# Batch 1's Fourier folds shared by two engines, with its last output a step sooner, and batch 0's q and k transposed in the banks of P

## The chip, the cores and the metric

The kernel runs on one core of a Trainium2 chip. The metric is the device time of one execution in microseconds (us). A core has five engines that run beside each other, each with its own queue of instructions in program order: PE (TensorE, matrix products), ACT (ScalarE), DVE (VectorE), POOL (GpSimd) and SP (SyncE, which here issues transfers). They wait for each other by semaphores. Matrix products land in PSUM, which this kernel deals out in banks; everything else lies in SBUF.

## The reference

Attention over 8 batches and 8 heads, with 576 tokens of 64 channels, keeps only the 32 largest scores of each row. Its output goes through a two-dimensional Fourier transform of which only the real part is used, and then through a normalised two-layer MLP.

```python
scores = scale * np.matmul(q, k.transpose(0, 1, 3, 2))          # 8 x 8 x 576 x 576
kth = np.partition(scores, -32, axis=-1)[..., -32:-31]
scores = np.where(scores >= kth, scores, -1e9)
attn = softmax(scores)                                          # written out in the reference
x = np.matmul(attn, v)  ->  (8, 576, 512)                       # heads side by side
u = x + real(fft(fft(x, axis=1), axis=2))
un = (u - mean(u)) / sqrt(var(u) + 1e-6)                        # over the 512 channels
out = u + relu(un @ w_ch1) @ w_ch2                              # 512 x 2048 and 2048 x 512
```

The two weights arrive as float64 and are turned into float32 on the chip.

## The kernel before, in words

**Tiles and steps.** The scores are cut into 288 tiles: 8 batches, 4 pairs of heads a batch, 9 tiles a pair, 36 tiles a batch. A tile is 128 rows of one head by 576 keys; the fifth tile of a pair (token block 4) holds the 64 last rows of both heads. One outer loop makes one step per tile. In step i DVE runs the second half of tile i's top-k and the first half of tile i + 1's: each half is two rounds of MAX8 (eight largest values, L349) and MATCH_REPLACE8 (L351, strikes them out). A step's seven such operations take about 5.08 us.

**The life of a tile.** PE forms the scores (`sp`, and the tails `sp_t`), ACT copies them to S (L302, L331). After DVE's last MAX8, POOL's `bounds` makes `nt` (L358), two numbers a row from the largest and the 32nd value. `mask` is one ACT operation (L365, into `wk`) and one of POOL (L366): it leaves kept scores as they are and pushes the others far down. `expo` is ACT's exp with its row sum (L372). PE transposes the result in a bank of `ps_t` (`tpP`, L393; tails `tpP_t`), ACT copies it to PT (L396 to L408), and after the fifth and ninth tile of a pair PE multiplies with v (`o`, L430). ACT copies that to xT (L444), PE turns it back to tokens (`tpx`, L475), and DVE divides by the row sums (`normalise`, L479) into `x`, one tensor per batch. From batch 1 on, a tile is masked one step after its top-k, transposed two steps after it, and the multiplication (`attend`, `attended`) comes three steps after.

**The Fourier part of a batch** begins when its last tile has reached `x`. Tokens and channels are folded first, so that the transforms are shorter. A fold is made for each parity (par 0 and 1, even and odd frequencies) by `fold_ops`: `first` adds or subtracts the halves of the tokens (a copy to `sd`, one operation on 128 x 1024, one on 32 x 512), `second` the halves of the channels (128 rows: two operations on 2 x 256; 32 rows: two on 256; into `zw`), `third` the quarters (into `fg`; for 128 and for 32 rows each a memset, two small copies and four operations on 127 columns a block). The 32 rows are the tails. All tensor operations of the folds have line L521. Then `dft_tokens` multiplies with tables on PE (`yp`, L579, two banks of `ps_m`, tag "mm", for each parity; ACT copies to `y`), and `dft_channels` makes `mp` (L635). The sum goes to `u`, which is normalised and transposed to `unT` (`tpu`). The arrival of a batch's MLP in the queue is the last of these steps.

**Where the folds run.** In batch 0 all are on DVE, one parity after the other. In batch 1 all are on POOL, in steps 76 and 77 (par 0), 79 and 80 (par 1), with the multiplications `yp` in steps 78 and 81. In batches 2 to 6 all are on POOL over more steps. In the last batch DVE has par 0 and POOL par 1.

**The MLP** of a batch is cut into units: `hidden` (`hp`, L721, then relu on ACT) and `back` (`cp`, L745, two row blocks of w2 a unit). They are put between the steps of the next batch. `level` spreads what is in the queue evenly over the steps up to the next arrival, using a table of costs for the fixed work (`fixed_cost`), so a step gets more units where it has less other work or where the next arrival is nearer.

**What sets the order.** A plan keyed by step and place: `at(step, where, fn)`. PE's and ACT's part comes first ("convert", "act", "pe1", "pe2", "pe"), then the top-k on DVE, then "pool0" on POOL, then `bounds(i)`, then "dve", then "pool", "load" and the rest. Within an engine the program's order is the engine's order. So what lies in "pool0" of step i stands ahead of nt(i) on POOL, and what lies in "dve" of step i stands behind that step's top-k and ahead of the next.

**Batch 0** has no MLP beside it. In its steps the weights are converted: `split` on DVE (L162, L165) writes two banks of `ps_m` ("wm", "we"), ACT converts (L177 to L184), POOL joins three times a chunk (L192) and later subtracts means (L892; they come from `centre` on PE, L886). Its own q and k are transposed by `prep` (`tpq`, `tpk`, L247; ACT's copies L255 to L260), once each per pair.

**PSUM banks:** `ps_s` two (scores, means), `ps_t` two (`tpP`, and tpq and tpk from batch 1 on), `ps_o` one (`o`, and tpx from batch 1 on), `ps_m` three ("mm": everything else, among it wm, we, tpq and tpk of batch 0, `yp`, `mp`, `hp`, `cp`).

Of the kernel before, what the change touches and what calls it, by code (L numbers as in the profile page):

```python
# [18 lines left out]
P = 128  # L19
TH = 32  # L20
# [39 lines left out]
def kernel(  # L60
# [174 lines left out]
            load_full(v_of[pair], v, pair)  # L235
            load_tails(v_of[pair], v, pair, (0, TAIL))

    def prep(n, pair, pool=ps_t, tag="tp"):

        if pair >= NPAIR:  # L240
            return 0.0
        src = nat.pop((n, pair))
        t_sb = attp.tile([P, S if n == "q" else NF * P], F32, name=f"{n}T_{pair}", tag=f"{n}T")
        for c0, c1 in ((0, NF), (NF, NC)):
            tp = pool.tile([P, 4, P], F32, name=f"tp{n}_{pair}_{c0}", tag=tag)
            for c in range(c0, c1):
                nc.tensor.transpose(  # L247
                    tp[:, c - c0, :], src[:, c, :, :].rearrange("p h d -> p (h d)"), ident
                )
            if c0 == 0:  # L250
                dst, got = t_sb[:, 0:NF * P], tp.rearrange("p a c -> p (a c)")
            else:
                dst, got = t_sb[:, NF * P:], tp[:, 0, 0:TAIL]
            if n == "q":
                nc.scalar.mul(out=dst, in_=got, mul=scale)  # L255
            elif c0 == 0:
                nc.scalar.copy(out=dst, in_=got)
            else:
                for hd in (slice(0, D), slice(D, P)):
                    nc.scalar.copy(out=kt_t[hd, hd], in_=got[hd])  # L260
        (qT_of if n == "q" else kT_of)[pair] = t_sb
        return 0.7
# [234 lines left out]
    def two(ap):  # L497
        return ap.rearrange("p (m two) -> p two m", two=2)
# [3 lines left out]
    PARTS = [(slice(0, P), slice(0, 2)), (slice(0, TH), slice(2, 3))]  # L502
    folded, y_of, yt_of, us_of, rs_of, unT_of = ({} for _ in range(6))

    def fold_ops(b, par, eng, space="own"):

        x = x_of[b]

        if space == "hT":
            sp = batp.tile([P, NIT * CW[0]], F32, name=f"fsp_{b}", tag="hT")

        def buf(n, name):
            if space == "hT":
                return sp[:, 3 * DM * n:3 * DM * (n + 1)].rearrange("p (s c) -> p s c", s=3)
            pool, tag = (batp, ("fold_s", "fold_d")) if space == "own" else (attp, ("PT0", "PT1"))
            return pool.tile([P, 3, DM], F32, name=f"{name}_{b}_{par}", tag=tag[n % 2], bufs=1)

        def tt(o, a, b, op):  # L520
            eng.tensor_tensor(out=o, in0=a, in1=b, op=op)  # L521

        def first():
            sd = buf(0, "sd")
            folded[b, par] = [sd]
            op0 = ALU.add if par == 0 else ALU.subtract

            if eng is nc.vector:
                nc.vector.tensor_copy(out=sd[0:TH, 2, :], in_=x[TH:TAIL, 4, :])
            else:  # L530
                nc.scalar.copy(out=sd[0:TH, 2, :], in_=x[TH:TAIL, 4, :])
            tt(sd[:, 0:2, :], x[:, 0:2, :], x[:, 2:4, :], op0)
            tt(sd[0:TH, 2, :], x[0:TH, 4, :], sd[0:TH, 2, :], op0)

        def second():
            sd = folded[b, par][0]
            zw = buf(1, "zw")
            folded[b, par].append(zw)
            for pp, ss in PARTS:
                s_, z_ = sd[pp, ss], zw[pp, ss]  # L540
                tt(z_[:, :, 0:Q2], s_[:, :, 0:Q2], s_[:, :, Q2:DM], ALU.add)
                tt(z_[:, :, Q2:DM], s_[:, :, 0:Q2], s_[:, :, Q2:DM], ALU.subtract)

        def third(n):
            if n == 0:
                fg = buf(2, "fg")
                folded[b, par].append(fg)
            _, zw, fg = folded[b, par]
            for pp, ss in PARTS:
                z_, f_ = zw[pp, ss], fg[pp, ss]  # L550
                if n == 0:
                    eng.memset(f_[:, :, Q1:Q1 + 1], 0.0)
                    eng.tensor_copy(out=f_[:, :, 0:DM:Q2], in_=z_[:, :, 0:DM:Q2])
                    up, down = slice(1, Q1), slice(Q2 - 1, Q1, -1)
                    tt(f_[:, :, up], z_[:, :, up], z_[:, :, down], ALU.add)
                    tt(f_[:, :, Q1 + 1:Q2], z_[:, :, up], z_[:, :, down], ALU.subtract)
                else:
                    up, down = slice(Q2 + 1, Q3), slice(DM - 1, Q3, -1)
                    tt(f_[:, :, up], z_[:, :, up], z_[:, :, down], ALU.subtract)
                    tt(f_[:, :, Q3:DM - 1], z_[:, :, up], z_[:, :, down], ALU.add)  # L560
                    eng.tensor_copy(out=f_[:, :, DM - 1:DM], in_=z_[:, :, Q3:Q3 + 1])

        return [first, second, lambda: third(0), lambda: third(1)]

    def dft_tokens(b, par):

# [337 lines left out]
    for b in range(B):  # L904
        end = PER_BATCH * (b + 1) - 1
        last = b == B - 1
        first, soon = b == 0, b == 1
        T0 = end + (2 if first else 4)
        if first:

            def folds(b=b):
                for par, space in ((0, "own"), (1, "hT")):
                    for op in fold_ops(b, par, nc.vector, space):
                        op()
            at(T0, "dve", folds)
            ft, fc = (T0 + 1, T0 + 1), T0 + 1
        elif soon:

            for par in range(2):
                def folds(par=par, b=b, T0=T0):  # L920
                    for n, op in enumerate(fold_ops(b, par, nc.gpsimd)):
                        at(T0 + 3 * par + n // 2 + 1, "pool0", op)
                at(T0, "begin", folds)
            ft, fc = (T0 + 3, T0 + 6), T0 + 7
        elif not last:
            for par in range(2):
                def folds(par=par, b=b, T0=T0):
                    for n, op in enumerate(fold_ops(b, par, nc.gpsimd)):
                        at(T0 + (6 if par else 1) + n, "pool0", op)
                at(T0, "begin", folds)  # L930
            ft, fc = (T0 + 5, T0 + 11), T0 + 12
        else:
            def folds(b=b):
                a = fold_ops(b, 0, nc.vector)
                for op in a + fold_ops(b, 1, nc.gpsimd, "PT"):
                    op()
            at(T0, "dve", folds)
            ft, fc = (T0 + 1, T0 + 3), T0 + 4
# [61 lines left out]
    while i < N + 4 or plan or queue:  # L1000
# [8 lines left out]

        fixed, j = [], i + 3  # L1010
        e = items[j][2] if j < N else None
        preps, bank = [], (ps_m, "mm") if short else (ps_t, "tp")
        if i < N and i % PER_PAIR == 0:
            preps.append(lambda: prep("q", pair_of + 1, *bank))
        if i < N and i % PER_PAIR == 5:
            preps.append(lambda: prep("k", pair_of + 1, *bank))
        fixed.append(lambda: scores(j - 1, 1) if e == 1 else scores(j, 0))
        n_mask = 0
        fixed += preps
# [48 lines left out]
        if short:  # L1068
            if piece is not None and r in (4, 8) and i < PER_BATCH:

                out_next.append(lambda pc=(pair, r // 8): attended(*pc, late_next))
                pending.append((i + 1, pair, r // 8))
        elif PER_BATCH <= i - 3 < N:
            pair, r = divmod(i - 3, PER_PAIR)
            if r in (4, 8):
                cost += attend(pair, r // 8)
                attended(pair, r // 8, late_next)
# [64 lines left out]
```

## Time and profile before

| | |
|---|---|
| time, median of 5 runs | 2014.59 us (2013.58 to 2016.05) |
| the profiled execution, its own time | 2016.83 us |
| its span in the profile | 2015.0 us |
| mean granted TensorE clock | 0.953 |
| PE busy | 1872.2 us, 93% |
| DVE busy | 1630.1 us, 81% |
| ACT busy | 1220.8 us, 61% |
| POOL busy | 844.6 us, 42% |

The span is what the profile shows; 1.8 us of the execution lie outside it. Times in the timelines count from the start of the span. A line of a timeline reads: start, duration of the instruction or group, engine, line, operation, out <- in, shapes, count, and in brackets the idle time of the engine just before and what ended it. PEld is the loading of weights into PE, which overlaps its products. The granted clock is the share of full speed that the throttle gave PE. Batch 0's steps end near 265 us; batch 1's last tile has its maxima near 475 us, its folds lie between 501 and 541 us in the trace before. A row named "128x512" on POOL or DVE with a count of 4 holds several operations of unlike shapes in a row; the groups by form keep them apart.

### The profile page before, as it was taken

What the parts mean: (1) busy time and instruction counts of PE and PEld (TensorE: products, weight loads), DVE (VectorE), ACT (ScalarE), POOL (GpSimd) and SP (SyncE); (2) the same over time, 40 slices, a digit from 0 to 9 for tenths busy, and PEclk for the clock granted to TensorE, in tenths of its full rate; (3) what the DMA queues carried; (4) which work ended last, traced back from release to release, by engine and by line L of the source; (5) the groups of instructions that cost most, each with busy time, mean ns of one, the idle gap of its engine ahead of it and who ended that gap; (6) DMA issues with size and microseconds to landing.
All of it is one profiled execution on the core that took longest, in us unless ns stands there. A gap on an engine that the chain in (4) does not pass through costs nothing.

```text
span 2015.0 us, 27503 instructions
## 1 busy us (share of the span) xinstructions
PE 1872.2 (93%) x8626; PEld 1132.7 (56%) x8626; DVE 1630.1 (81%) x3381; ACT 1220.8 (61%) x3008; POOL 844.6 (42%) x1138
## 2 busy tenths in 40 slices
PE   5666689999799999999999999999999999998999
PEld 3334356565465655646565556647565656565655
DVE  7998898999799998988889888988899888853100
ACT  6877737676576666656666667656666667541100
POOL 4869822333643365234533274235532364223000
PEclk9677679999899999999999999999999999998999
DMA  4323100010000101001000001010000001000000
GB/s 127 96 84 98 54 7 19 24 26 24 24 19 24 27 19 28 15 21 27 24 21 15 27 19 29 18 32 14 22 24 24 20 15 32 0 14 1 11 14 11
DMA packets 133585, 57.82 MB, mean 29 GB/s; under 512 B 124352, under 2 KB 124480, under 8 KB 133440
## 3 DMA queue, kind: packets, MB, share of 16 engines
q1 hardware_dynamic: 132208, 55.73, 10.3%
q8 instruction: 69, 1.13, 0.2%
q14 instruction: 76, 0.62, 0.1%
q10 hardware_dynamic: 1232, 0.33, 0.1%
HBM read 46.57 MB, written 9.44 MB: 28 GB/s over the span
## 4 chain that ended last, share of the span: by engine, by line
PE 69%; DVE 14%; POOL 5%; ACT 5%; issue 5%; DMA 0%; SPq 0%; POOLq 0%; DVEq 0%; ACTq 0%
PE cp L745 20%; PE hp L721 19%; PE o L430 6%; DVE m L349 6%; PE sp L328 5%; DVE wk L351 5%; PE tpP L393 5%; PE yp L579 3%; PE cp L781 2%; PE mp L635 2%; POOL wk L366 2%; PE sp_t L298 1%; POOL w L192 1%; PE cm L886 1%; ACT wk L365 1%
## 5 line engine op out<-in xcount | busy, mean ns | idle before, releaser
L366 POOL TENSOR_TENSOR wk<-S,wk 128x576 f32<-128x576 f32 x288 | 406.3, 1411 | 881.8 <-ACT wk L365 841.5
L349 DVE MAX8 m<-wk 128x8 f32<-128x576 f32 x864 | 623.1, 749 | 5.5
L721 PE MATMUL hp<-unT,w 128*128 128x256 f32 (+1 forms) x2048 | 540.6, 411 | 4.0 <-POOL t L683 2.2
L745 PE MATMUL cp<-w,hT 128*128 128x512 f32 x1024 | 478.8, 599 | 0.0
L721 PEld LDWEIGHTS hp<-unT,w 128*128 128x128 f32 x2048 | 375.3, 191 | 126.4 <-issue 32.2
L351 DVE MATCH_REPLACE8 wk<-m,wk 128x576 f32<-128x576 f32 x576 | 427.6, 742 | 0.0
L745 PEld LDWEIGHTS cp<-w,hT 128*128 128x128 f32 x1024 | 179.6, 191 | 183.4 <-issue 182.6
L372 ACT ACTIVATE wk<-wk,nt 128x576 f32<-128x576 f32 x288 | 225.0, 781 | 66.6 <-POOL wk L366 65.4
L365 ACT ACTIVATE wk<-S,nt 128x576 f32<-128x576 f32 x288 | 226.5, 786 | 48.9 <-POOL nt L358 46.7
L349 DVE MAX8 m<-S 128x8 f32<-128x576 f32 x288 | 214.1, 743 | 35.6 <-ACT S L302 35.3
L396 ACT COPY PT<-tpP 128x512 f32<-128x512 f32 (+1 forms) x320 | 170.8, 545 | 119.0 <-PE tpP L393 116.6
L393 PE MATMUL tpP<-ident,wk 128*128 128x128 f32 x1152 | 187.2, 287 | 54.9 <-ACT wk L372 49.1
L393 PEld LDWEIGHTS tpP<-ident,wk 128*128 128x128 f32 x1152 | 140.4, 146 | 155.7 <-ACT wk L372 72.6
L725 ACT ACTIVATE hT<-hp 128x320 f32<-128x320 f32 (+1 forms) x256 | 104.6, 409 | 200.7 <-PE hp L721 198.7
L351 DVE MATCH_REPLACE8 wk<-m,S 128x576 f32<-128x576 f32 x288 | 213.7, 742 | 0.0
L430 PE MATMUL o<-PT,v 128*64 128x256 f32 (+3 forms) x1440 | 196.0, 416 | 10.3 <-ACT PT L396 9.8
L331 ACT COPY S<-sp 128x512 f32<-128x512 f32 (+1 forms) x264 | 141.7, 588 | 68.8 <-PE sp L328 68.6
L328 PE MATMUL sp<-kT,qT 64*128 64x512 f32 (+1 forms) x528 | 168.2, 692 | 2.3 <-ACT means L896 1.9
L430 PEld LDWEIGHTS o<-PT,v 128*64 128x64 f32 x1440 | 111.8, 154 | 84.4 <-ACT PT L396 14.8
L192 POOL TENSOR_TENSOR w<-w,space 128x512 f32<-128x512 f32 x96 | 123.4, 1286 | 4.4 <-ACT space L183 1.7
L759 DVE SCALAR_TENSOR_TENSOR x<-cp,gi,x 128x512 f32<-128x512 f32 x11 | 8.2, 746 | 128.3 <-PE cp L745 128.3
L479 DVE TENSOR_TENSOR x<-tpx,rd 128x256 f32<-128x256 f32 x64 | 27.1, 424 | 77.2 <-PE tpx L475 74.7
(124 smaller groups left out, 1912.8 us busy)
## 6 DMA issues: line engine op xcount, KB each, us to landing
space<-in_moe_w_ch_dram SPq DMA_DIRECT2D x32, 512.0 KB, 3.5
nat<-in_q_dram SPq DMA_DIRECT2D x128, 64.0 KB, 2.0
v<-in_v_dram SPq DMA_DIRECT2D x128, 64.0 KB, 2.1
out_dram<-x SPq DMA_DIRECT2D x32, 256.0 KB, 2.0
nat<-in_k_dram SPq DMA_DIRECT2D x124, 64.0 KB, 2.0
nat<-in_q_dram SPq DMA_DIRECT2D x128, 8.0 KB, 1.7
v<-in_v_dram SPq DMA_DIRECT2D x128, 8.0 KB, 1.7
nat<-in_k_dram SPq DMA_DIRECT2D x124, 8.0 KB, 1.6
```

Of the source, the lines that this page charges most:

```text
L192: nc.gpsimd.tensor_tensor(out=dst, in0=dst, in1=(low, high, ex)[part], op=ALU.mult if part else ALU.add,)
L328: nc.tensor.matmul(sp[r], lhsT=qT[hd, q_cols], rhs=kT[hd, :], start=True, stop=True)
L349: ops.append(lambda src=src, m8=m8: nc.vector.max(out=m8, in_=src))
L351: ops.append(lambda src=src, m8=m8: nc.vector.match_replace(w, m8, src, NEG))
L365: nc.scalar.activation(out=w, in_=Ssb[i], func=AF.Relu, scale=-FAR, bias=Nt[i][:, 1:2])
L366: nc.gpsimd.tensor_tensor(out=w, in0=Ssb.pop(i), in1=w, op=ALU.subtract)
L372: nc.scalar.activation(out=w, in_=w, func=AF.Exp, bias=Nt.pop(i)[:, 0:1], accum_out=den_t[pair % 3][:, c:c + 1],)
L393: nc.tensor.transpose(tp[:, c, :], p_sb[:, k0 + P * c:k0 + P * (c + 1)], ident)
L396: nc.scalar.copy(out=pt[:, NF * he:NF * (he + 1), col:col + w], in_=tp[:, :, o:o + w])
L430: nc.tensor.matmul(o[D * e:D * (e + 1), c0:c1], lhsT=vv[:, c, e, :], rhs=pt[:, 2 * NF if c == NF else NF * e + c, c0:c1], start=(c == 0), ...
L721: nc.tensor.matmul(hp[:, 0:w], lhsT=w1[:, dt, P * it:P * (it + 1)], rhs=unT[:, dt, 0:w], start=(dt == 0), stop=(dt == NDT - 1),)
L745: nc.tensor.matmul(cp, lhsT=hT[:, it, P * n:P * (n + 1)], rhs=w2[:, it, :], start=(it == 0), stop=(it == NIT - 1),)
```

## The change

**Batch 1's folds** are dealt out. `fold_ops` takes two engines, one for the 128 rows and one for the 32 (`eng[0]`, `eng[1]`), and optionally one for the whole second stage (`mid`). For batch 1 POOL has the first stage's and the third stage's 128 rows; DVE has the first stage's tail, all of the second stage and the third stage's tails. The copy to `sd` ("moved") stays on ACT, in "act" of steps 74 and 78. POOL's first lies in "pool0" of steps 75 and 78, DVE's whole share in "dve" of the same steps, POOL's third in "pool0" of steps 76 and 79. Per parity, DVE gets 12 more instructions, and POOL's fold instructions fall from 20 to 8. `T0` is one step earlier, so the two `yp` stand in steps 77 and 80, the channel transforms and the arrival of batch 1's MLP are one step earlier too (step 85), and batch 0's units are spread over 46 steps and no longer 47, batch 1's over 42 and no longer 41.

**Batch 1's last output** is multiplied one step sooner: `attend` and `attended` of tile 71 run in step 73, right behind its own transposes, its tpx in step 74, its normalisation at the end of DVE's step 74.

**Batch 0's q and k** (`prep` in steps 0 to 36) are transposed in the two `ps_t` banks ("tp") that `tpP` uses, and no longer in the three "mm" banks. For the other batches nothing of this differs.

On each engine the order changes with it. On PE both `yp` of batch 1 now stand ahead of the transposes of the tile in their step; on ACT the copies of `kT` come behind the mask of tile 76 and the copies of `y` ahead of PT of tile 75 and the exp of tile 76; on SP three stores of output stand ahead of a group of loads of v and k.

```diff
-    def prep(n, pair, pool=ps_t, tag="tp"):
+    def prep(n, pair):
...
-            tp = pool.tile([P, 4, P], F32, name=f"tp{n}_{pair}_{c0}", tag=tag)
+            tp = ps_t.tile([P, 4, P], F32, name=f"tp{n}_{pair}_{c0}", tag="tp")
...
-    def fold_ops(b, par, eng, space="own"):
+    def fold_ops(b, par, eng, space="own", mid=None):
...
+        def moved():
+            out, in_ = place(0)[0:TH, 2, :], x[TH:TAIL, 4, :]
+            if eng[1] is nc.vector and eng[0] is nc.vector:
+                nc.vector.tensor_copy(out=out, in_=in_)
             else:
-                nc.scalar.copy(out=sd[0:TH, 2, :], in_=x[TH:TAIL, 4, :])
...
+                nc.scalar.copy(out=out, in_=in_)
+
+        def first(p):
+            sd, op = place(0), ALU.add if par == 0 else ALU.subtract
+            if p == 0:
+                eng[0].tensor_tensor(out=sd[:, 0:2, :], in0=x[:, 0:2, :], in1=x[:, 2:4, :], op=op)
+            else:
+                s_ = sd[0:TH, 2, :]
+                eng[1].tensor_tensor(out=s_, in0=x[0:TH, 4, :], in1=s_, op=op)
+
+        def second(p):
+            pp, ss = PARTS[p]
+            s_, z_ = place(0)[pp, ss], place(1)[pp, ss]
+            for cols, op in ((slice(0, Q2), ALU.add), (slice(Q2, DM), ALU.subtract)):
+                (mid or eng[p]).tensor_tensor(
+                    out=z_[:, :, cols], in0=s_[:, :, 0:Q2], in1=s_[:, :, Q2:DM], op=op
+                )
+
+        def third(n, p):
+            pp, ss = PARTS[p]
+            z_, f_ = place(1)[pp, ss], place(2)[pp, ss]
+
+            def tt(out, up, down, op):
+                eng[p].tensor_tensor(out=f_[:, :, out], in0=z_[:, :, up], in1=z_[:, :, down], op=op)
...
-        T0 = end + (2 if first else 4)
+        T0 = end + (2 if first else 3 if soon else 4)
...
             for par in range(2):
-                def folds(par=par, b=b, T0=T0):
-                    for n, op in enumerate(fold_ops(b, par, nc.gpsimd)):
-                        at(T0 + 3 * par + n // 2 + 1, "pool0", op)
+                def folds(par=par, b=b, T1=T0 + 1 + 3 * par):
+                    f = fold_ops(b, par, (nc.gpsimd, nc.vector), mid=nc.vector)
+                    at(T1 if par else T1 - 1, "act", f["moved"])
+                    at(T1, "pool0", lambda: f["first"](0))
+                    at(T1, "dve", lambda: [
+                        f["first"](1), f["second"](0), f["second"](1),
+                        f["third"](0, 1), f["third"](1, 1),
+                    ])
+                    at(T1 + 1, "pool0", lambda: [f["third"](n, 0) for n in range(2)])
                 at(T0, "begin", folds)
             ft, fc = (T0 + 3, T0 + 6), T0 + 7
...
-        preps, bank = [], (ps_m, "mm") if short else (ps_t, "tp")
+        preps = []
         if i < N and i % PER_PAIR == 0:
-            preps.append(lambda: prep("q", pair_of + 1, *bank))
+            preps.append(lambda: prep("q", pair_of + 1))
...
-        elif PER_BATCH <= i - 3 < N:
-            pair, r = divmod(i - 3, PER_PAIR)
+        soon_tile = 2 * PER_BATCH - 1
+        for tile in (i - 3, i - 2):
+            if not PER_BATCH <= tile < N or (tile == i - 2) != (tile == soon_tile):
+                continue
+            pair, r = divmod(tile, PER_PAIR)
             if r in (4, 8):
                 cost += attend(pair, r // 8)
                 attended(pair, r // 8, late_next)
```

## The prediction

> **What bounds the kernel now.** Read first the page's slices of 50.4 us, the eleventh (504 to 554 us) above all.
>
> ```profile
> PE   5666689999799999999999999999999999998999
> ...
> POOL 4869822333643365234533274235532364223000
> PEclk9677679999899999999999999999999999998999
> ```
>
> From the seventh slice on, PE is full except here and near the end. So PE sets the time, and the hole at batch 1's folds is what a change there can win. The windows of 50 us (columns: length; busy time and instructions of PE, PEld, DVE, ACT, POOL; granted clock; DMA share; GB/s) give its size:
>
> ```profile
> 450.00:500.00 50.00, 49.58 (x224) 27.61 (x223) 49.04 (x105) 34.11 (x86) 15.55 (x19) 1.00 0.10 24
> 500.00:550.00 50.00, 38.50 (x180) 24.16 (x179) 39.66 (x80) 26.24 (x70) 34.91 (x53) 0.86 0.10 24
> 600.00:650.00 50.00, 50.00 (x222) 27.93 (x221) 49.05 (x104) 33.58 (x86) 15.95 (x20) 1.00 0.10 24
> 150.00:200.00 50.00, 33.90 (x142) 19.80 (x141) 44.41 (x87) 38.89 (x88) 46.90 (x45) 0.70 0.33 98
> ```
>
> PE lacks 11.5 us, and its clock falls to 0.86: the second yp (536.84 to 543.85) took 7.0 us, the first 5.2. Two things follow. After 600 PE has no hole, so microseconds won at 540 reach the end. And DVE is at 49 of 50 just before: work moved to it isn't free. In batch 0 (150 to 200) POOL is the fullest engine. Next, PE's timeline in the hole; the bracket is the idle time ahead and what released it:
>
> ```profile
> 510.59 0.66 PE L393 MATMUL tpP<-ident,wk 128*128 128x128 f32 x4 [3.87 <-ACT kT L257]
> ...
> 521.77 1.12 PE L393 MATMUL tpP<-ident,wk 128*128 128x128 f32 x4 [2.39 <-ACT wk L372]
> ...
> 534.99 1.07 PE L247 MATMUL tpq<-ident,nat 128*128 128x128 f32 x5 [4.42 <-ACT PT L396]
> 536.84 4.63 PE L579 MATMUL yp<-fs,fg 128*128 128x145 f32 x16 [0.79 <-POOL fg L521]
> ```
>
> Three waits of 10.7 us, all named after ACT. But ACT itself waited 5.79 us at 509.29 and 4.39 at 533.69 for nt, a tiny operation of POOL. POOL's timeline says why:
>
> ```profile
> 500.36 1.41 POOL L366 TENSOR_TENSOR wk<-S,wk 128x576 f32<-128x576 f32 x1 [3.83 <-ACT wk L365]
> 501.72 2.37 POOL L521 TENSOR_TENSOR sd<-x 128x1024 f32<-128x1024 f32 x1
> 504.04 1.26 POOL L521 TENSOR_TENSOR sd<-x,sd 32x512 f32<-32x512 f32 x1
> 505.26 3.85 POOL L521 TENSOR_TENSOR zw<-sd 128x512 f32<-128x512 f32 x4
> 509.08 0.18 POOL L358 TENSOR_TENSOR nt<-m,cc 128x2 f32<-128x2 f32 x1
> ```
>
> Tile 76's maxima were ready at 501.97 (the end of its last MAX8), yet its nt stood behind 7.4 us of folds until 509.08. Then come 4.97 us of third fold (511.49 to 516.46) ahead of nt(77). Parity 1 is alike: nt(79), ready at 517.97, ran at 533.47.
>
> **The change, part by part.** *Folds leave POOL.* Per parity POOL had 7.45 + 4.97 = 12.4 us. It keeps the 2.37 of the first and the 128 rows of the third, 0.10 + 0.19 + 1.41 + 1.4 (the second pair like the first) + 0.18, about 3.1: 5.5, with a nt between them. So nt's cover falls from 7.4 and 5.0 us to 2.4 and 3.1.
>
> *They arrive on DVE.* Batch 0's folds run there, and parity 1's (274.72 to 281.28) have no POOL work beside them. By form (count, busy us, mean ns):
>
> ```profile
> L521 DVE TENSOR_TENSOR zw<-sd 32x256 f32<-32x256 f32 x2 | 1.9, 1008 | 0.0
> ...
> L521 DVE TENSOR_TENSOR fsp<-fsp 32x256 f32<-32x256 f32 x2 | 0.7, 405 | 0.0
> ```
>
> Alone: 32x512 0.67, two 128x2x256 1.34, two 32x256 0.81, tails 4 x 0.27 plus two copies and a memset 0.3: 4.2 us per parity, 8.4 in all, on an engine that idles 13.3 us in 495 to 585. Queued behind DVE's middle piece is the next tile's top-k. The middle waits for POOL's first: top-k of step 75 ends at 497.7, L366(74) about 499.0 (495.2 before, plus the 3.8 that two units of 1.88 take when batch 0's MLP spreads over 46 steps rather than 47), first over by 502.1 with 0.8 for the handover. So DVE stands some 3.8 us once; in parity 1 first is done before DVE gets there.
>
> *What both engines at once cost* is the disputed price. The two lines of form above are the same operation: 1.01 with a POOL L366 beside it, 0.405 without. Summed, batch 0's first parity lost 2.1 us beside two L366 (zw 3.15 against 1.94, two 32x127 1.68 against 0.47). In batch 7 both engines fold:
>
> ```profile
> 1825.02 3.26 DVE L521 TENSOR_TENSOR sd<-x 128x1024 f32<-128x1024 f32 x1
> ...
> 275.17 1.23 DVE L521 TENSOR_TENSOR fsp<-x 128x1024 f32<-128x1024 f32 x1
> ...
> 1824.62 2.57 POOL L521 TENSOR_TENSOR sd<-x 128x1024 f32<-128x1024 f32 x1 [20.68 <-DVE x L479]
> ```
>
> There a parity on DVE took 16.3 us (1824.58 to 1840.88) against 6.5 alone. So bounds per parity: 0; 2.1; and, scaled by 16.3/6.5, 4.2 x 2.5 - 4.2 = 6.3. I take 2.1: POOL has one L366 and one third beside DVE's ops, with waits between, as in batch 0, not back-to-back folds. The Trainium skill, "SBUF — State Buffer", section "SBUF: two separate sides", speaks against the change: it says that a DVE operation with two SBUF inputs and a GpSimd operation exclude each other for a whole instruction over a shared port pair. Batch 7's 3.26 agrees with it; taken strictly it gives the 6.3 end, that is the first rival's time.
>
> *When the second yp starts.* Now 536.84. Without collisions: DVE's folds end 502.1 + 3.5 = 505.6 (first's tail goes earlier); tile 77's maxima come 8.6 later (3.5 of a step, one of 5.08), 514.2; nt to tpP takes 5.3 there (516.46 to 521.77) plus 0.1, so tpP(77) at 519.6; then tpP, o, sp, a unit, transposes, 8.8 before (521.77 to 530.57): 528.4. Parity 1's folds (step end 520.8 + 4.2, third 526) don't hold it. With 2.1 per parity and POOL's pieces 1 longer: 531.5. Serialised: DVE's folds run to 511 and 534.8, yp at 534.5.
>
> *Steps moved.* Tile 71's o, tpx and normalise come a step sooner, both yp before the next transposes: tpP(78), sp_t and tpq (0.6 + 0.3 + 0.4 + 1.1, 2.3 us) now stand behind the second yp, so they come off the gain; tpx earlier gives 0.55. o_1 may wait about 1 us for PT's copies, paid in the 499.0. On ACT kT's copies fall behind L365(76) and the y copies ahead of PT(75) and exp(76), 1 to 2 us beside PE's yp. On SP three stores pass a load of v and k; DMA share is 0.10, price 0. Gain: 536.84 - 531.5 - 2.3 + 0.55 = 3.6, and the second yp at a clock like the first's, 7.0 - 5.2 = 1.8: 5.4.
>
> *Does DVE's delay come back?* It is then about 3.8 + 2 x (4.2 + 2.1) = 16.4 later, less what it idles, 13.3 in part. Tile 86, the tightest, has 3.9 us between maxima and tpP beyond the shortest chain of 3.5, and two hp units (4.4) come before it: 8.3. So up to 8.3 of delay costs nothing.
>
> *Batch 0's transposes.* They leave the three mm banks, so DVE's splits stop waiting (waits view, 150 to 262: total, times, longest):
>
> ```profile
> DVE we L165 <- ACT kT L257: 5.2, 2, 2.7
> DVE wm L162 <- ACT space L179: 3.1, 2, 2.7
> DVE we L165 <- ACT qT L255: 2.1, 1, 2.1
> ```
>
> 10.4 us, but where POOL is busy 46.9 of 50 and never waits for DVE; at the end:
>
> ```profile
> 265.15 0.42 DVE L479 TENSOR_TENSOR x<-tpx,rd 128x256 f32<-128x256 f32 x1 [0.55 <-PE tpx L475]
> ```
>
> DVE already waits 0.55 there, so it is worth at most that. Against it tpP shares two banks with tpq and tpk and waits for their copies: steps 18, 32, 36 +0.7, +0.4, +0.7; 23 and 27, where PE's fifth transpose no longer waits, -0.7 each. Sum +0.3 (bounds -1.5 and +1.8). If POOL weren't the cover, the 10.4 would count.
>
> Sum: 5.4 - 0.3 = 5.1 less. The profiled execution, 2016.83 us (span 2015.0), stands 2.2 above the median of 2014.59; the difference carries over: 2009.5. A measurement tells 0.2% (4.0 us) from nothing: faster is below 2010.6, slower above 2018.6.
>
> **Rivals.** A: *the engines exclude each other as in batch 7.* For: 3.26 against 1.23, and POOL's third runs right beside DVE's tails. Against: in batch 0 most folds keep their price. yp at 534.5: 2.3 - 2.3 + 0.55 = 0.6; less 0.3: 2014.3.
>
> B, slower: *DVE becomes the bound.* The moved work 8.4, the wait of 3.8, exclusion 2 x 6.1: 24.4. DVE's idle time is itself waiting (for S 1.78 and 2.66, for tpx 5.61); if half of the 13.3 isn't there when needed, DVE is 24.4 - 6.7 = 17.7 late at tile 86, 9.4 past its cover, and A's gain of 0.3 is little against it: 2014.6 + 9.1 = 2023.7. It decides from 8.3 us of delay. Against: full exclusion needs POOL busy all along, and it has 5.5 us a parity.
>
> C, faster still: *no collisions.* yp at 528.4: 8.4 - 2.3 + 0.55 = 6.7, the clock 2.5 (PE's waits under 2.4 us), and batch 0 at 0: 9.2, so 2005.4. The trace speaks against it with the 1.01.
>
> D: *the hole closes only in name*, the waits moving behind yp to tpP(78) or to sd's copy on ACT (POOL waited 1.87 for it at 528.42): within A's time.
>
> **How the numbers follow.** Forecast 0.47, its own range 2007 to 2012.5, of which 0.42 is below 2010.6. A with D 0.26, B 0.13, C 0.14. Faster 0.42 + 0.14 = 0.56, same 0.05 + 0.26 = 0.31, slower 0.13. The range leaves out B and the fastest third of C, 0.18: 2003.0 to 2018.5.
>
> **What would show it.** nt(76) right after tile 76's maxima; second yp near 531.5; DVE's 32x256 folds at 0.4 (C), 0.5 to 1.0 (forecast), over 1.2 (A, B); PE above 42 of 50 in 500 to 550 with a clock over 0.9; no split waiting for kT or qT in 150 to 262; new waits of PE's tpP for those copies. Wrong: tpP of tiles 84 to 88 waiting for exp, with DVE at 49 of 50 from 500 to 600 (B), or batch 0's end, x at 265.15, moved by over 2 us.

## The result, and the profile after

The changed kernel took 2010.51 us (median of 24 runs, 2009.00 to 2011.87), the kernel before 2015.31 us in the runs beside them (42 runs, 2013.48 to 2017.02): ratio 0.9977, interval 0.9972 to 0.9983. That is 4.8 us less; 5.1 were forecast. Run once more beside four other kernels it took 2011.63 us, ratio 0.9980 (0.9971 to 0.9989). The profiled execution took 2009.00 us, its span is 2007.1 us. It is the fastest of its 24 runs, while the profiled execution before was one of the slowest of its own, so the 7.8 us between the two profiles are not the effect.

The page's slices of 50.2 us (PE, POOL, granted clock):

```profile
PE   5667689999889999999999999999999999997999
...
POOL 4879822324433365234532374225533364223000
PEclk8777689999999999999999999999999999998999
```

The hole in the eleventh slice has become two shallower slices, and POOL's 6 there is a 4. The windows of 50 us, same columns as before:

```profile
500.00:550.00 50.00, 42.66 (x238) 28.62 (x236) 49.55 (x102) 31.86 (x84) 24.83 (x33) 0.93 0.10 24
550.00:600.00 50.00, 43.73 (x202) 28.05 (x202) 48.05 (x106) 31.74 (x82) 16.39 (x33) 0.93 0.08 19
```

PE is busy 4.2 us more in the first window than before, and 5.1 less in the second, which was nearly full before (48.84). DVE is now full, 49.55 where it had 39.66. PE's timeline between 500 and 570 says what became of the three waits:

```profile
506.31 0.66 PE L393 MATMUL tpP<-ident,wk 128*128 128x128 f32 x4 [0.80 <-ACT kT L257]
514.42 0.65 PE L393 MATMUL tpP<-ident,wk 128*128 128x128 f32 x4 [1.95 <-ACT wk L372]
521.16 3.82 PE L605 MATMUL yp<-fs,fg 128*128 128x145 f32 x16 [2.19 <-POOL fg L558]
529.24 0.76 PE L247 MATMUL tpq<-ident,nat 128*128 128x128 f32 x5 [1.24 <-ACT PT L396]
568.15 1.12 PE L393 MATMUL tpP<-ident,wk 128*128 128x128 f32 x4 [5.63 <-ACT kT L257]
```

The waits of 3.87 and 4.42 us are 0.80 and 1.24, and the second yp starts at 521.16 instead of 536.84. But a wait of 5.63 us is new, at tile 84, where the kernel before had none. Its cause is in POOL's and ACT's timelines:

```profile
504.79 0.19 POOL L358 TENSOR_TENSOR nt<-m,cc 128x2 f32<-128x2 f32 x1 [2.19 <-PE yp L605]
...
559.79 0.20 POOL L708 TENSOR_TENSOR t<-gi 128x5 f32<-128x5 f32 x1 [3.57 <-DVE gi L704]
...
564.11 1.40 POOL L366 TENSOR_TENSOR wk<-S,wk 128x576 f32<-128x576 f32 x1
```
```profile
565.54 0.78 ACT L372 ACTIVATE wk<-wk,nt 128x576 f32<-128x576 f32 x1 [6.91 <-POOL wk L366]
```

The first line is nt(76), 0.1 us after tile 76's maxima (504.71): that queue is cured. The others are new. The inverse square root of batch 1 begins with three operations on DVE and goes on with sixteen small ones on POOL, 4.3 us, queued ahead of L366 of tile 84. DVE is late, so POOL stands 3.57 us for it, and tile 84's mask, done by ACT at 557.0, is finished by POOL only at 565.5.

### The profile page after: what moved, and what is told of

It reads as the page before. It is cut to its first block, busy times and chain, and to the rows that moved or that the text cites. A ratio compares the mean times of both kernels' runs of the same rounds, so it can differ in the third digit from the quotient of the medians.

```text
span 2007.1 us, 27513 instructions
## 1 busy us (share of the span) xinstructions
PE 1864.9 (93%) x8626; PEld 1128.9 (56%) x8626; DVE 1641.8 (82%) x3405; ACT 1221.0 (61%) x3008; POOL 832.0 (41%) x1114
## 3 DMA queue, kind: packets, MB, share of 16 engines
q1 hardware_dynamic: 132208, 55.73, 10.4%
## 4 chain that ended last, share of the span: by engine, by line
PE 67%; DVE 16%; issue 6%; POOL 5%; ACT 5%; DMA 0%; SPq 0%; POOLq 0%; DVEq 0%
PE hp L747 20%; PE cp L771 20%; DVE m L349 7%; PE o L430 6%; DVE wk L351 5%; PE tpP L393 5%; PE sp L328 5%; PE yp L605 3%; POOL wk L366 2%; PE cp L807 2%; PE mp L661 2%; PE sp_t L298 1%; POOL w L192 1%; ACT wk L365 1%; PE cm L912 1%
## 5 line engine op out<-in xcount | busy, mean ns | idle before, releaser
L366 POOL TENSOR_TENSOR wk<-S,wk 128x576 f32<-128x576 f32 x288 | 407.5, 1415 | 863.4 <-ACT wk L365 835.1
L365 ACT ACTIVATE wk<-S,nt 128x576 f32<-128x576 f32 x288 | 226.3, 786 | 49.2 <-POOL nt L358 47.0
```

The source lines that it names most:

```text
L365: nc.scalar.activation(out=w, in_=Ssb[i], func=AF.Relu, scale=-FAR, bias=Nt[i][:, 1:2])
L366: nc.gpsimd.tensor_tensor(out=w, in0=Ssb.pop(i), in1=w, op=ALU.subtract)
```

## Experiments

Each kernel ran beside the kernel before, and each ratio is against those runs (medians 2014.86, 2015.61, 2015.58 and 2015.36 us in the four sets). Since the runs of one kernel spread over 3 us and more, each profile was also cut into stages: from the start of tpP of tile 38 (batch 0 is over) to that of tile 144 (batches 1 to 3 are over), called the stage below, and on to the end of the last matmul (cp). These are differences of times in the traces, and each kernel but the changed one has a single trace.

| kernel | ratio, interval | tile 38 to 144 | first yp of last batch to the end of its last | tile 38 to last cp |
|---|---|---|---|---|
| before | 1 | 609.30 | 20.84 | 1699.38 |
| changed, two traces | 0.9977 and 0.9980 | 604.92, 604.99 | 21.11, 21.08 | 1695.24, 1695.32 |
| batch 0's banks only | 1.0001, 0.9992 to 1.0010 | 609.07 | 20.81 | 1699.14 |
| folds and sooner, old banks | 0.9992, 0.9983 to 1.0001 | 605.98 | 20.79 | 1696.03 |
| sooner, all folds on POOL | 0.9987, 0.9978 to 0.9995 | 602.79 | 23.78 | 1695.82 |
| shared, not sooner | 1.0002, 0.9994 to 1.0010 | 609.14 | 20.78 | 1699.17 |
| middle piece on POOL | 1.0000, 0.9992 to 1.0009 | 608.48 | 21.06 | 1698.78 |
| all folds on DVE | 1.0002, 0.9992 to 1.0011 | 608.43 | 21.03 | 1698.74 |
| late inverse square root | 0.9978, 0.9969 to 0.9987 | 602.64 | 23.85 | 1695.76 |
| that, k's copies first | 0.9981, 0.9973 to 0.9990 | 602.58 | 23.91 | 1695.73 |
| that, mask behind k | 0.9983, 0.9974 to 0.9992 | 602.56 | 23.86 | 1695.69 |
| that, 2.2 us added | 0.9995, 0.9986 to 1.0004 | 602.64 | 24.69 | 1698.33 |
| that, last folds on DVE | 0.9915, 0.9901 to 0.9929 | 602.60 | 17.31 | 1682.30 |

**Batch 0's banks alone.**

```diff
-        preps, bank = [], (ps_m, "mm") if short else (ps_t, "tp")
+        preps, bank = [], (ps_t, "tp")
```

> The kernel before, with batch 0's q and k transposed in the banks of P and nothing else of the change. Theory 1 (the traces): batch 0 is where half of the gain is. In the trace after, tile 36 is transposed at 290.63, in the trace before at 294.40; of the 3.8 us some 3.5 should stay, so about 2011.8 us. Theory 2 (the recorded working): the waits of DVE that vanish, 10.4 us, lie beside a busier POOL, and PE's tpP waits for the copies of q and k: 0.3 more, 2015.6 us. If theory 2 holds, the 3.8 us of the two traces are the scatter of single executions (2013.5 to 2017.0 for the kernel before).

2015.01 us against 2014.86. Theory 2 holds: no gain, and the forecast's 0.3 lies in the interval (1.8 us either way). The 3.8 us at tile 36 were scatter; this kernel's own trace has tile 36 at 294.38, where before had it at 294.40, and the changed kernel's second trace at 294.12.

**The rest of the change alone**, with the old banks:

```diff
...
-        preps = []
+        preps, bank = [], (ps_m, "mm") if short else (ps_t, "tp")
...
```

> The changed kernel with batch 0's q and k back in the three mm banks; folds shared and last output a step sooner as changed. Theory 1: what is left of the 4.8 us of the whole change without batch 0's 3.5: 1.3 us less than before, 2014.0 us. Theory 2 (the recorded sum): the folds give 5.4 us, 2009.9 us. In both the second yp of batch 1 starts about 12 us earlier in batch 1's own time than before.

2014.12 us; by the ratio 1.6 less than before, and the interval, 0.2 more to 3.4 less, excludes the forecast's 5.4 and holds theory 1's 1.3. By stages it is 3.35 us faster from tile 38 on (1699.38 - 1696.03), at the edge of that interval; the trace is that of its fastest run (2011.03 us). The 1.0 us from its stage to the changed kernel's 604.95 is a window of half clock at 795.6, in batch 3, which the changed kernel's traces don't have. Up to tile 124, ahead of that window, the two parts add up: 3.29 us here and 0.18 by the banks alone, against 3.41 in the changed kernel.

**The earlier step without sharing.**

```diff
-                    f = fold_ops(b, par, (nc.gpsimd, nc.vector), mid=nc.vector)
...
+                    for n, op in enumerate(fold_steps(fold_ops(b, par, (nc.gpsimd,) * 2))):
+                        at(T0 + 3 * par + n // 2 + 1, "pool0", op)
```

> The changed kernel, but all of batch 1's folds on POOL as before, in pool0 of steps 75, 76, 78 and 79; the last output a step sooner, the earlier yp and batch 0's banks stay. Theory 1: the sharing is what fills PE's hole, the earlier step alone leaves nt of tiles 75, 76, 78 and 79 behind 7.5 and 5.0 us of folds, so PE's idle time between 490 and 560 stays 10 us or more: about the time of the kernel with batch 0's banks alone, 2012 us (2010.5 to 2014). Theory 2: the earlier step does it, PE's idle time there falls to 5 us, and DVE isn't late, so there is no wait for the inverse square root: 2007 us or less.

2012.47 us, as theory 1 said. PE waited 2.74, 0.89, 2.49, 3.51 and 0.89 us here, 10.5 in all. But the stage says the reverse of theory 1: from tile 38 to 144 this is the faster one, 602.79 against 604.95, since DVE is not late and tile 84 has no wait. It loses 2.7 us again in the last batch's yp (23.78 against 21.1). From tile 38 to the last cp the two traces are then 0.6 us apart (1695.82 and 1695.24); by the runs the changed kernel is some 2 us the faster, and the traces do not show where the rest lies.

**Sharing without the earlier step.**

```diff
-        T0 = end + (2 if first else 3 if soon else 4)
+        T0 = end + (2 if first else 4)
...
-        soon_tile = 2 * PER_BATCH - 1
+        soon_tile = -1
```

> The changed kernel with the folds shared but nothing sooner: the last output of batch 1, its folds, its yp and its MLP's arrival stay in the steps of the kernel before; batch 0's banks as changed. Theory 1: the step sooner is worth 1.5 to 2.5 us (the kernel with all folds on POOL and the step sooner was 2.6 us faster than before) and sharing the rest, so 2012.5 us, with PE's gap of 1.5 us at tile 42 and the unit's place of before. Theory 2 (the recorded sum, in which the step sooner gave 0.55 and sharing the rest): 2010.5 to 2011 us.

2014.67 against 2015.61 us, and a ratio of 1.0002: nothing. Theory 1 was nearer and still 2 us off. The second yp starts at 527.01, and then PE waits 2.64 us for x at 550.45 and 3.08 at 573.06 for an exp. So by the runs sharing alone wins nothing, the earlier step alone 2.6 us, the two together 4.0 to 4.8.

**Where the 4.4 us of the stage lie.** The traces can be cut further, at tile 74 (just ahead of the folds) and tile 92 (behind the hole), and at tile 124. The differences to the kernel before, in us (less than 0 is faster):

| tiles | changed | folds and sooner, old banks | sooner, all folds on POOL | late inverse square root | shared, not sooner | banks only |
|---|---|---|---|---|---|---|
| 38 to 74 | -0.23 | -0.21 | -0.22 | -0.23 | +0.03 | +0.05 |
| 74 to 92, the folds | -0.10 | +0.02 | -1.92 | -2.43 | +1.10 | -0.20 |
| 92 to 124 | -3.08 | -3.10 | -3.10 | -3.09 | +0.03 | -0.03 |
| 124 to 144 | -0.96 | -0.03 | -1.27 | -0.91 | -1.33 | -0.06 |

The stretch of the folds, in the kernel before and then in the changed one, with the columns of the windows above:

```profile
500.20:617.49 117.29, 104.62 (x517) 67.63 (x516) 103.52 (x217) 74.32 (x190) 62.34 (x98) 0.94 0.08 18
```
```profile
496.19:613.39 117.20, 103.59 (x522) 67.54 (x520) 114.45 (x242) 73.95 (x190) 47.49 (x73) 0.94 0.08 18
```

It has become 0.1 us shorter. PE's idle time in it grew from 12.7 to 13.6 us, and less half clock gave 1.0 back. POOL lost 15 us of work and DVE gained 11. Counted from tile 38, tile 82 came 8.8 us earlier than before, but tile 84 was 0.3 later. With the earlier step, sharing costs 1.8 us here against leaving all folds on POOL.

The rows 38 to 74 and 92 to 124 belong together: a unit of 2.2 us of PE's work has moved from the second into the first, and PE's idle time fell by 2.4 and 0.8 us. These 3.3 us come with the earlier step, whichever engine folds, and are missing without it. They lie far from the folds, so the spread of the MLP's units, which the earlier step changes, is the likely cause; no run changes the spread alone.

The last row is mostly one window of half clock, 3.41 us at 801.6 in the trace before, around a wait of PE of 1.61 us. At the same place PE waits 1.95 us in the changed kernel, and the clock does not fall. The window is there in two kernels with the earlier step (the old banks, the middle piece on POOL) and missing in one without it (shared, not sooner), so it can't be put down to the shared folds or the earlier step.

**The middle piece back on POOL**, and **all of the folds on DVE**:

```diff
-                    f = fold_ops(b, par, (nc.gpsimd, nc.vector), mid=nc.vector)
+                    f = fold_ops(b, par, (nc.gpsimd, nc.vector))
```
```diff
...
+                    for op in fold_steps(fold_ops(b, par, (nc.vector,) * 2)):
+                        at(T1, "dve", op)
```

> The changed kernel with the 128 rows of the second stage back on POOL (two operations of 1.4 us a parity, behind nt of tiles 75 and 78); DVE keeps the tails, 2.9 us a parity instead of 4.2. Theory 1: DVE's delay is what costs after the folds (the gap of 5.6 us at tile 84), so 1.3 us less a parity makes that gap 2 to 3 us smaller, while L366 of tiles 75 and 78 come 2.7 us later on POOL, which PE has cover for: 2009 us. Theory 2: POOL's queue is still the tighter one, nt and L366 come later and PE's gaps ahead of tpP of tiles 75 to 79 grow by the 2.7 us each: 2013 us.

> The changed kernel with all of batch 1's folds on DVE, in the same steps: 6.5 us a parity instead of 4.2, and none on POOL. It is the recorded rival B, DVE as the bound, made stronger on the side of DVE's work and weaker on the side of collisions. Theory 1 (DVE's lateness is given back at tile 84): DVE is 2.3 us later a parity, less the 1.4 us a parity that its operations lost beside POOL's in the trace after and its wait for POOL's pieces, so tile 84's gap grows from 5.6 to 6 to 8 us and the time is 2011 to 2013 us. Theory 2 (collisions and the hand-over between the engines cost more than the work): 2009 us or less, and PE's wait of 2.2 us ahead of the second yp is gone.

Both are no faster than before (2014.63 and 2015.94 us). With the middle on POOL the wait at tile 84 stayed 5.66 us, so theory 1 fell; PE's wait for PT rose from 1.24 to 2.54 us as theory 2 has it, and 16.1 us of PE's work in the stage again ran at half clock, against 10.7 (3.4 of them in the window at tile 124). The time is 1.6 us above theory 2's. With all on DVE neither theory's time came. The wait for fg ahead of the second yp stayed (2.21 us), and so did the one at tile 84:

```profile
575.63 1.12 PE L393 MATMUL tpP<-ident,wk 128*128 128x128 f32 x4 [5.57 <-ACT kT L257]
```

That gap did not grow, but the tiles from 76 to 85 came later than in the changed kernel, tile 84 by 4.3 us counted from tile 38. This is rival B in the flesh, at a price of no gain rather than 9 us lost.

**The inverse square root four steps later.**

```diff
-        at(s + 1, "begin" if quick else "dve", lambda b=b: rsqrt(b))
+        at(s + (5 if soon else 1), "begin" if quick else "dve", lambda b=b: rsqrt(b))
```

> The changed kernel, with batch 1's inverse square root (three operations of DVE, sixteen of POOL) four steps later, in step 88; the MLP needs it only at the end of its first row block. In the trace after, POOL waited 3.57 us for DVE's gi and then spent 4.4 us on the sixteen operations ahead of L366 of tile 84, ACT's exp waited 6.91 for that, and PE stood 5.63 us ahead of tpP of tile 84. Theory 1: that order is the cause and what the shared folds win is given back there: 4 to 5 us faster than the changed kernel, about 2006 us, and PE's gap near 562 is gone. Theory 2: DVE's lateness itself holds tiles 84 to 86 (their maxima come 1.9 us earlier at most than before): the gap moves to tpP of 85 or 86, and the time stays within 1 us of 2010.5.

In the stage it won 2.3 us (604.95 to 602.64), all of it in the stretch of the folds, half of what theory 1 said. ACT and PE show the other half:

```profile
565.67 0.78 ACT L365 ACTIVATE wk<-S,nt 128x576 f32<-128x576 f32 x1 [4.31 <-POOL nt L358]
```
```profile
567.30 1.11 PE L393 MATMUL tpP<-ident,wk 128*128 128x128 f32 x4 [3.04 <-ACT kT L257]
```

exp of tile 84 is done at 561.1 now, but the bank that tpP needs is freed by ACT's copy of kT, and that stands behind L365 of tile 85, whose maxima come from the late DVE. Yet the time is 2011.18 us, no better than the changed kernel. Two kernels, both with the late inverse square root, took that queue order away, one edit each:

```diff
-        fixed += preps
+        fixed = preps + fixed if i == 2 * PER_BATCH + 14 else fixed + preps
```
```diff
         fixed += preps
+        if i == 2 * PER_BATCH + 14:
+            n_mask = len(preps)
```

> The changed kernel with the inverse square root four steps later (as in the run before) and, in step 86 alone, k's transposes and ACT's copies of them ahead of the scores and of tile 85's mask. With the late inverse square root PE's gap near 564 fell from 5.6 to 3.0 us; the rest was named after ACT's kT copy, which stood behind L365, and that waited 4.31 us for maxima of a late DVE. Theory 1: two queue orders hold PE there, this takes the second: the gap falls under 1 us and the time to 2007.5 us (2006 to 2009.5). Theory 2: DVE's lateness is the bound in 560 to 600 however the queues are ordered: the 3 us turn up again ahead of the next tpP, and the time stays at 2010.5 to 2011.5.

> The changed kernel with the late inverse square root and, in step 86, tile 85's mask behind k's transposes, so that ACT's copies of k no longer stand behind L365; the order on PE is the changed kernel's. Of the 3.0 us that PE still waited near 564, 1.3 to 3 should go. Two ways to count the time: from tile 38 to tile 286 the late inverse square root was 6.6 us shorter than before, but in the last batch its yp took 23.9 us and not 20.9 to 21.1, since the clock came back only 12.7 us after yp began (6.2 to 7.1 in the others). Theory 1 (the clock's grid decides the last batch, and runs are locked to that grid at the end of batch 0): 1.3 to 3 us more move the last yp out of that place on the grid, its time returns to 21, and the whole is 2007 to 2008 us. Theory 2 (the last yp is simply slow when the batches before it are fast): yp stays at 23.9, 2009.5 us.

(The first of them no longer computes the same: the tails of the scores made in step 86 are taken with the next pair's keys. Only its times are of use here.) They took 2011.88 and 2011.22 us. Theory 2 of the first holds for the stage: 602.58 and 602.56 us, the same to 0.1. So the 1.3 to 3 us that the second was to win did not come, and its last yp stayed at 23.9 us, as its theory 2 has it. PE's timeline of the second:

```profile
570.87 0.66 PE L393 MATMUL tpP<-ident,wk 128*128 128x128 f32 x4 [0.68 <-ACT wk L372]
...
576.25 0.66 PE L393 MATMUL tpP<-ident,wk 128*128 128x128 f32 x4 [2.24 <-ACT wk L372]
```

The 3.04 us come again as 0.68 and 2.24, ahead of the next two tpP. In both kernels a window of half clock at 567 is gone as well, and still the stage keeps its length, with a further wait of 1.75 us ahead of a later tpP: there DVE is the bound, whatever the queues.

**Where the 2.3 us went.** All three spend 23.9 us on the last batch's yp (five cp units lie between the two parities), against 21.1. Windows of 3.41 us of the kernel with the late inverse square root, soon after its first yp (1827.49), show why; the column ahead of the DMA share is the granted clock:

```profile
1829.96:1833.37 3.41, 2.73 (x11) 2.25 (x12) 2.19 (x8) 0.00 (x0) 2.57 (x5) 0.50 0.00 0
1833.37:1836.78 3.41, 3.41 (x14) 2.16 (x12) 0.00 (x0) 0.94 (x3) 0.00 (x0) 0.50 0.00 0
1836.78:1840.19 3.41, 3.41 (x4) 1.42 (x5) 0.00 (x0) 0.90 (x4) 0.00 (x0) 0.50 0.00 0
1840.19:1843.61 3.42, 3.42 (x9) 1.52 (x8) 0.00 (x0) 0.00 (x0) 0.00 (x0) 1.00 0.00 0
```

PE stood 8.71 us for fg, the clock fell to half, and came back 12.7 us after yp began; in the changed kernel after 7.0. In every trace all changes of the clock lie on one grid of 3.41 us, whose phase differs from trace to trace. Tile 38 falls in the same place on it each time: 1.68 and 1.72 us after a grid point with the old banks, 1.96 to 2.11 with the new. So by tile 38 the program is in step with the grid, perhaps because batch 0 spends much of its time at half clock (0.70 in 150 to 200); no run tests that. What comes later repeats: tile 144 to 286 took 881.91 to 881.96 us in all the kernels that change nothing there. Set out by where the last yp starts on the grid, with four traces in each group: 0.44 to 0.61 us after a point, yp took 20.8 us; 0.83 to 1.10, 23.8 to 23.9; 3.18 to 3.40, 21.0 to 21.1.

> The changed kernel once more, unaltered, beside the other kernels of this set, for the scatter of single profiles. In every trace so far the granted clock changes only on a grid of 3.41 us whose phase differs from run to run. If that phase is the scatter, this trace differs from the first one of the same kernel by up to 3 us at tile 38 (end of batch 0) and by up to 3.4 us in the last batch, with the same gaps of PE in batch 1 (0.8, 1.9, 2.2, 1.2 and 5.6 us between 500 and 570); the median stays at 2010.5 within 1 us. If the scatter is not the clock, the gaps themselves differ.

The second trace of the changed kernel has tile 38 1.8 us later than the first, the gaps 0.80, 1.95, 2.20, 1.24 and 5.65 us, and stage times within 0.1: the scatter is not in the gaps, though its last batch did not differ, since the place on the grid did not.

> The changed kernel with the late inverse square root and 2.2 us of work added on PE in batch 5: the scores of two tiles are computed twice into the same bank (four more matmuls of 64 x 512, 0.56 us each). Theory 1 (grid): tile 286 comes 2.2 us later against the kernel without the addition (4.4 ahead of the kernel before, no longer 6.6), which puts the last batch's yp where it stands in the changed kernel, so yp takes 21 us again and the 2.2 cost nothing: 2010.5 to 2011.2 us, the time without the addition. Theory 2 (no grid): 2.2 us slower, 2013.4 us.

```diff
...
+            for _ in range(2 if i in (200, 203) else 1):
...
```

2014.41 us: theory 1's forecast failed, and by the time theory 2's 2013.4 was the nearer. The addition took 1.74 us and not 2.2, so yp started 2.67 us after a grid point, a place that no trace had shown, and took 24.69 us. The loss in the trace, 2.6 us, is the 1.74 and 0.84 more in yp. Another place went with another time of yp, as in the groups above, but no run has yet foretold yp's time from its place; the rule by which the clock comes back is open, since here it stayed at half over three windows in which PE was busy throughout.

**The shared folds of the last batch undone**, on top of the late inverse square root:

```diff
-                for op in a + fold_steps(fold_ops(b, 1, (nc.gpsimd,) * 2, "PT")):
+                for op in a + fold_steps(fold_ops(b, 1, (nc.vector,) * 2, "PT")):
```

> The changed kernel with the late inverse square root and, in the last batch, both parities of the folds on DVE, one after the other, and none on POOL. In all traces so far the two engines fold side by side there, DVE's parity takes 16.3 us instead of 6.5, and PE waits 8.7 us for its first fg. Theory 1 (the engines exclude each other, so the shared form is the slower one): the first fg is there after 5.5 to 6 us and not 11.7, parity 1 after 13, long before PE asks for it; PE's wait falls to about 3 us. With the late inverse square root (tile 38 to 144 in 602.6 us) 5 to 6 us less in the last batch, and a yp that starts on a warmer clock: 2004 us (2002 to 2007). Theory 2 (the clock's grid takes it back): yp's own time grows by as much as it starts earlier, 2009 to 2011 us.

1998.63 us (5 runs), ratio 0.9915: 17 us faster than before and some 12 faster than the changed kernel, 3 better than the lower end of theory 1. PE's first yp, and DVE's first fold, of the changed kernel and then of this one:

```profile
1828.07 2.27 PE L605 MATMUL yp<-fs,fg 128*128 128x145 f32 x8 [8.71 <-DVE fg L558]
...
1816.85 3.26 DVE L540 TENSOR_TENSOR sd<-x 128x1024 f32<-128x1024 f32 x1
```
```profile
1821.98 2.36 PE L605 MATMUL yp<-fs,fg 128*128 128x145 f32 x16 [1.86 <-DVE fg L558]
...
1817.61 1.22 DVE L540 TENSOR_TENSOR sd<-x 128x1024 f32<-128x1024 f32 x1
```

Both parities, one after the other on DVE, are done 13.4 us after the start (1817.16 to 1830.53); side by side on two engines they took 16.3. PE waits 1.86 us and not 8.71, the clock does not fall there, and yp takes 17.31 us: 6.85 and 6.54 us against the kernel with the late inverse square root alone, together 13.4 of the 13.5 us between the two (1695.76 to 1682.30).

## Why the prediction was right, point by point

The time was right by luck. The forecast had all of its 5.4 us in PE's hole at the folds, and that stretch gave 0.1. What the earlier second yp won there, the wait at tile 84 took back. The 4.4 us of the stage are 3.3 that come with the earlier step, in stretches for which the forecast had no gain, 1.0 at a window of half clock in batch 3, and that 0.1. From tile 38 to the last cp it is 4.1 us in the traces; where the rest of the measured 4.8 lies is open.

**Nt out of POOL's queue**: right. nt(76) ran 0.1 us after its maxima, nt(79) likewise (525.49, 525.57).

**The price of two engines at once**: right, 2.2 us a parity for a forecast of 2.1. (The working's own two differences in batch 0, 3.15 - 1.94 and 1.68 - 0.47, add up to 2.4 and not 2.1.) DVE's fold operations in 495 to 523 of the trace after, by form, and then the same forms in the last batch of the last experiment, where POOL is idle:

```profile
L558 DVE TENSOR_TENSOR fg<-zw 32x127 f32<-32x127 f32 x8 | 3.9, 536 | 0.0
L549 DVE TENSOR_TENSOR zw<-sd 32x256 f32<-32x256 f32 x4 | 2.7, 707 | 0.0
```
```profile
L558 DVE TENSOR_TENSOR fg<-zw 32x127 f32<-32x127 f32 x8 | 1.9, 271 | 0.0
L549 DVE TENSOR_TENSOR zw<-sd 32x256 f32<-32x256 f32 x4 | 1.5, 406 | 0.0
```

Lost: 8 x 0.265 + 4 x 0.30 and, for the 32x512, 2 x 0.54 (1.21 against 0.67), 4.4 us over both parities. The 32x256 at 0.71 lie in the forecast's 0.5 to 1.0. Rival A is out for batch 1. The Trainium skill, "SBUF — State Buffer", section "SBUF: two separate sides", has one of the two engines wait for the other's whole instruction; batch 7's 3.26 against 1.22, and its end in the last experiment, agree with that, but in batch 1 the four 128x2x256 cost 0.67 us each as alone. POOL had no operation under way when three of them began, and where its L366 of tile 75 met one, POOL paid: that L366 took 2.15 us and not 1.41.

**The start of the second yp**: forecast 531.5, 5.3 us earlier than before; measured from tile 38 it came 11.9 us earlier (225.13 before, 213.22 after). The mis-sized term is L366(74), forecast 3.8 us later for two more units ahead of it; it ended 1.6 later (183.5 and 185.1 after tile 38). With it the 3.8 us that DVE was to stand for POOL's first fell away: DVE's first fold began at 495.41, as its top-k ended. And tpP(77) to yp took 6.7 us, not 8.8 or more.

**The spread of batch 0's units** was priced as a delay only. With it waits of PE of 1.48 us at 341.59 and 0.44 at 346.41 are gone, and others up to tile 124, 3.3 us in all. The forecast had no term for this, and it is the largest part of what was won.

**DVE's delay, said to cost nothing up to 8.3 us**: this step failed. The cover was counted on DVE, ACT and PE at tile 86. The delay came back at tile 84 by way of POOL, since sixteen small operations that wait for DVE stand there ahead of L366. The price was 5.63 us of PE, of which moving them got 2.3 back; the rest is DVE itself. One of the forecast's own signs of being wrong was there: DVE busy 49.55 and 48.05 of 50 us in 500 to 600, and tpP of tile 84 late behind an exp that waited 6.91 us.

**Clock**: 1.8 us forecast for the second yp; it took 5.9 us where it had taken 7.1. In the stage PE worked 16.0 us at half clock before and 10.7 after, worth 2.7; PE's idle time fell by 1.7 (20.7 to 19.0). Together they are the stage's 4.4. But 1.65 of the 2.7 belong to the window at 801.6, and the idle time fell by 3.3 away from the folds and rose by 0.9 at the folds and 0.6 at tile 124. So the forecast's mechanism, less waiting in PE's hole, gave nothing here; that stretch is 2.4 us shorter with the inverse square root moved, and 1.9 with the earlier step and no sharing at all.

**After 600 PE has no hole**: a misreading. In the trace before PE waits 1.61 us at 801.67, with a window of half clock, and 8.71 us at 1836.23, ahead of the last batch's first yp. The working names a hole near the end and leaves it there; the last experiment won 13.5 us in it.

**Batch 0**: 0.3 more forecast, within what was measured. That its 10.4 us of DVE's waits count for nothing, to within 1.8 us, is shown by the run with the banks alone.

**Rivals**: B's mechanism is real, and with all folds on DVE it takes the whole gain, and at the changed kernel's load it took back what the hole at the folds had won. D, a hole that closes only in name, comes nearest to what happened at the folds; it put the waits at tpP(78) or at sd's copy, and they came at tpP(84). C did not come.

## What to carry to other kernels

When work is moved from a full queue to another engine, follow that engine's delay through every queue that waits for it, the small operations too: sixteen of 0.2 us ahead of one mask were worth 2.3 us here. Two engines that share elementwise work can be slower than one of them alone, so try the one first, above all where it stands idle anyway. For effects under half a per cent compare stages of two traces that repeat, and ask of a gain that vanishes whether a later wait and the clock took it. When the time comes out as forecast, cut the trace at the place that was changed: here that place gave 0.1 of 4.8 us.

## What the runs showed of the hardware that was not expected

The granted clock changes only on a grid of 3.41 us, in all fourteen traces. In the two traces of the changed kernel every stage after batch 0 repeats to 0.1 us, while the runs of one kernel spread by 3.5 us (before, 2013.48 to 2017.02) and up to 7.6 (shared, not sooner). A gain of 2.3 us upstream went with a loss of 2.7 us in the last batch, where the clock came back 12.7 us after yp began and not 7.0. The Trainium skill, "TensorE: Matmul & The Clock Gate", section "What's actually happening", gives a free-running window of that length, which agrees; that everything after the first such window of work runs at the full clock does not agree with the traces, where the clock stayed at half over two and three windows in which PE was busy throughout.
